# Filling TensorE's gaps in the opening of a Fourier-mixing and SoLU kernel with unread products, and moving two groups of real products

## The chip, the cores and the metric

The kernel runs on one core of one Trainium2 chip. The metric is the device time of one execution in microseconds (us). Before the change three runs gave 1123.95, 1124.88 and 1125.96 us, a median of 1124.88. The profile comes from one further execution.

Names of engines: PE is TensorE's matmuls, PEld its weight loads, DVE is VectorE, ACT is ScalarE, POOL is GpSimd, SP is the engine that only issues DMAs. A line such as L217 is a line of the kernel file.

## The reference

```python
X = np.fft.fft(x, axis=1)            # x: 8 x 3136 x 256
X = np.fft.fft(X, axis=2)
x = X.real.reshape(8 * 3136, 256)
h = x @ w_in                         # 256 x 1024
e = np.exp(h - max(h)); sm = e / (sum(e) + 1e-9)
solu = h * sm
ln = (solu - mean(solu)) / np.sqrt(var(solu) + 1e-6) * g_ln
out = ln @ w_out                     # 1024 x 256
```

Maximum, sum, mean and variance are taken over each row of 1024. The weights arrive in 64-bit floats, and the kernel itself turns them into 32-bit floats.

## The kernel before

The transform over the 3136 positions is split as 49 x 64. The eight batches are worked on in four pairs. The first pair's first transform is the opening of the kernel. It runs in eight **chunks** `c` = 0 to 7, one per turn of the loop `for c in range(NC)` (L823). In each turn DVE adds the mirrored half (`add_mirror`, L145 and L147) and folds the features into a tile `y` (`fold`: L152, L153, L165). PE then makes two products per chunk (`transform1`, L217; in the last chunk there is a small third tile `y0`). ACT copies each result out of PSUM (L220) into a tile `z`, and SP writes `z` to a DRAM tile `zd` (`keep`, L225). There are two `y` tiles in turn, so chunk `c` can only be folded once PE has read chunk `c - 2`. A product of 32-bit floats shows in the trace as two matmul instructions, called passes here: a chunk is 8 passes of some 256 columns.

DVE and ACT also convert the weights in the same loop: DVE takes `w_in` apart and puts it together (`exponent_in`, `narrow_in`, L586 to L636), with three ACT steps between (`confine`, L610 to L614). `w_out` follows after chunk 7 (`exponent_out`, `narrow_out`), in four pieces, into `Wo`. Piece 0 and 1 fill `Wo[:, 0:4]`, which is what the first half of the mean row reads.

The second matrix `Wi` is the Fourier matrix `Q` over the features times `w_in`. PE makes it with `product_in` (L690): `h` = 0 and `h` = 1 are four products of 512 columns each, numbered 0 to 3 by `parts`, and so is the middle row (`h` = KD = 2). Products `h` = 0 and the middle row use PSUM tile `h0`, `h` = 1 uses `h1`. ACT copies them out (`keep_in`, L694). The middle row's left operand lies in `w_mid`, written by ACT in `mid` (L681).

After the loop, `turn` (L233) reads `zd` back with the axes exchanged into a tile `g`: four DMAs on SP for the first two of five columns, four on POOL for the other three. `transform2` (L245) multiplies `g` by a table, ACT copies the result to `q` (L251), and `up` (L281) multiplies `q` by `Wi`: 4 passes of 512 columns into `h0`, 4 into `h1`. This is the start of a **unit**; there are 100 of them, as a rule with two tiles of 128 tokens each. On DVE a unit goes through `even` (L294), `join` (L302), `product` (L317), with ACT's `expo` (L310) and `square` (L324).

The program is under a manual schedule: each engine runs its instructions in the order in which the code issues them, and only semaphores between engines hold it up. So on PE everything behind a waiting matmul waits too.

`mean_out(0)` (L737) is four products of a matrix of ones by `Wo[:, 0:4]` into PSUM bank 3. It is the first half of the sum that `centre` later subtracts. `mean_out(1)` adds the second half after the first unit. In the kernel before, `mean_out(0)` stands after `begin(0)`, that is, behind unit 0's two `up`s and the `transform2` of unit 2, and ahead of `begin(1)`, which holds unit 1's `up`.

Of the kernel before, what the change touches and what calls it, by code (L numbers as in the profile page):

```python
# [9 lines left out]
FP32 = mybir.dt.float32  # L10
# [7 lines left out]
P = 128  # L18
# [26 lines left out]
def kernel(  # L45
# [19 lines left out]
    nc = tc.nc  # L65
    B, S, D = x.shape
    FF = moe_w_in.shape[1]
# [16 lines left out]
    ps_h = ctx.enter_context(tc.tile_pool(name="ps_h", bufs=1, space=PSUM))  # L84
# [11 lines left out]
    ident = const.tile([P, P], FP32, name="ident")  # L96
# [9 lines left out]
    def result(i):  # L106

        return banks[i % 4]
# [9 lines left out]
    def load(pr, c, room=None):  # L118

        r = slice(pr.p * PR, (pr.p + 1) * PR)  # L120
        rows = PR if pr.p else P
        if room is None:
            xa = xpool.tile([P, CH, D], FP32, tag="xa", name="xa")
            xb = xpool.tile([P, CH, D], FP32, tag="xb", name="xb")
        else:
            xa, xb = (t.rearrange("p (l d) -> p l d", d=D) for t in room)
        nc.sync.dma_start(out=xa[0:rows], in_=x_pn[r.start : r.start + rows, c * CH + 1 : (c + 1) * CH + 1, :])
        i = pr.p * NC + c
        nc.gpsimd.indirect_dma_start(
            out=xb[0:rows].rearrange("p l d -> p (l d)"), out_offset=None, in_=x_g,  # L130
            in_offset=bass.IndirectOffsetOnAxis(ap=idx[0:rows, i : i + 1], axis=0))
        xa, xb = xa[0:PR], xb[0:PR]
        x0 = None
        if c == NC - 1:
            x0 = xpool.tile([PR, 1, D], FP32, tag="x0", name="x0", bufs=1)
            nc.sync.dma_start(out=x0, in_=x_pn[r, 0:1, :])
        pr.raw[c] = (xa, xb, x0)

    def add_mirror(pr, c, engine, part=None):

        xa, xb, _ = pr.raw[c]
        rows = (0, CH) if part is None else (part * CH // 2, (part + 1) * CH // 2)
        r = slice(rows[0], min(rows[1], CH - 1 if c == NC - 1 else CH))
        a, rb = xa[:, r, :], xb[:, ::-1, :][:, r, :]
        i = engine.tensor_tensor(out=a[:, :, 1:D], in0=a[:, :, 1:D], in1=rb[:, :, D - 1 : 0 : -1], op=ALU.add)  # L145
        if part is None:
            engine.tensor_tensor(out=a[:, :, 0:1], in0=a[:, :, 0:1], in1=rb[:, :, 0:1], op=ALU.add)  # L147
        return i
# [6 lines left out]
    def fold(pr, c):  # L155

        xa, _, x0 = pr.raw.pop(c)
        pr.y[c] = xpool.tile([PR, CH, D], FP32, tag="y", name="y")
        sides = [(pr.y[c], xa)]
        if c == NC - 1:  # L160
            pr.y0 = xpool.tile([PR, 1, D], FP32, tag="y0", name="y0", bufs=1)
            sides.append((pr.y0, x0))
        for o, i in sides:
            fold_features(o, i)
            nc.vector.tensor_copy(out=o[:, :, 0:129:128], in_=i[:, :, 0:129:128])  # L165
# [21 lines left out]
    def transform1(pr, s):  # L187

        c, l = divmod(2 * s, CH)
        if s == 0:
            pr.zd = dram.tile([ZR, NH, D], FP32, tag="zd", name="zd")
        if l == 0:

            if pr.p or c < 2:
                pr.z = zpool.tile([ZR, CH, D], FP32, tag="z", name="z")
            elif c < 6:
                if c == 2:
                    pr.z_v = fpool.tile([P, 2, FF, 2], FP32, tag="v", name="z_v", bufs=2)  # L200
                pr.z = pr.z_v[0:ZR].rearrange("p a f b -> p (a f b)").rearrange("p (c l d) -> p c l d", c=4, l=CH)[:, c - 2]
            elif c == 6:
                pr.z = S_tiles[1][0:ZR, 0:2].rearrange("p a c k -> p (a c k)").rearrange("p (l d) -> p l d", l=CH)
            else:
                pr.z = gpool.tile([P, KG, D], FP32, tag="g", name="z_g")[0:ZR, 0:CH, :]
            pr.zs[c] = pr.z
        y = pr.y[c]
        ps = result(0 if pr.p else s).rearrange("p (l d) -> p l d", l=2)
        if s == NH // 2 - 1:
            parts = [(ps[0:ZR, 0], y[:, l], 0), (ps[0:ZR, 1], pr.y0[:, 0], 1), (ps[0:ZR, 1], y[:, l + 1], 2)]  # L210
        else:
            parts = [(ps[0:ZR], y[:, l : l + 2], 0)]
        pr.done.append(s)
        first = True
        for o, i, t in parts:
            for h, cs in enumerate((EVEN, ODD)):
                nc.tensor.matmul(o[..., cs], F[:, 2 * t + h, :], i[..., cs], start=first, stop=True,  # L217
                                 skip_group_check=True)
                first = False
        nc.scalar.copy(pr.z[:, l : l + 2, :], ps[0:ZR])  # L220
        if l == CH - 2:
            keep(pr, c, slice(0, ZR if pr.p else 4 * KG))
# [12 lines left out]
    def transform2(pr, k1, bank=0):  # L235

        i, k = divmod(k1, KG)
        g = pr.g[i]  # L240
        table = T[0][:, :, k, :] if i == 0 else T[1][:, :, k1 - KG, :]
        ps = result(bank)[:, 0 : KD * P]
        for h in range(KD):
            o = ps[:, h * P : (h + 1) * P].rearrange("p (b k) -> p b k", b=2)
            nc.tensor.matmul(o, g[:, k, h * P : (h + 1) * P], table,  # L245
                             start=(h == 0), stop=True, skip_group_check=True)
        return ps
# [324 lines left out]
    NW = 512  # L572
# [25 lines left out]
    def confine(unit, here=False, parts=(0, 1, 2)):  # L598

        if unit is None:  # L600
            return
        if here:
            bits(unit, unit, -896.0, ALU.add, 0.0, ALU.max)
            bits(unit, unit, 255.0, ALU.min, 2.0 ** 23, ALU.mult)
            return

        u = unit.bitcast(FP32)
        for i in parts:
            if i == 0:
                nc.scalar.activation(out=u, in_=unit, func=ACT.Relu, bias=limits[:, 0:1])  # L610
            elif i == 1:
                nc.scalar.activation(out=u, in_=u, func=ACT.Relu, bias=limits[:, 1:2], scale=-1.0)
            else:
                nc.scalar.activation(out=unit, in_=u, func=ACT.Identity, bias=limits[:, 2:3], scale=-(2.0 ** 23))  # L614
# [24 lines left out]
    class Weights:  # L639
# [43 lines left out]
        def product_in(self, h, parts=range(4), ps=None):  # L683
# [6 lines left out]
                nc.tensor.matmul(ps[:, fs], lhsT, self.w_in[c][:, fs], start=(c == 0), stop=(c == KD - 1))  # L690
            return ps

        def keep_in(self, h, ps):
            nc.scalar.copy(w_mid if h == KD else Wi[:, h, :], ps)  # L694

# [95 lines left out]
    with tc.manual_schedule():  # L791
        pairs = [Pair(p) for p in range(NP)]
        first, weights = pairs[0], Weights()
# [29 lines left out]
        for c in range(NC):  # L823

            if c == 0:
                weights.narrow_in(0)
                weights.narrow_in(1)
            elif c == 1:
                weights.narrow_in(2)
            add_mirror(first, c, nc.vector)  # L830
            if c == 0:
                weights.exponent_in(2)
            fold(first, c)
            if c == 1:
                weights.exponent_in(3)
            elif c == 2:
                weights.narrow_in(3)
            if c == NC - 1:
                for i in range(2):
                    weights.exponent_out(i)  # L840
                confine(weights.units[0], True)
                weights.narrow_out(0)
            if c + 6 < NC:
                load(first, c + 6)
            if c == 3:
                weights.place_out()
                for i in range(2):
                    weights.load_out(i)
                weights.load_table(0)
                weights.scale_out()  # L850
            for s in range(CH // 2):
                if c == NC - 1:
                    confine(weights.units[0], parts=(s,))
                transform1(first, c * CH // 2 + s)
            if c == 3:
                weights.mid()
            elif c == 5:
                weights.keep_in(0, weights.product_in(0))
            elif c == 6:
                odd = weights.product_in(1, (0, 1))  # L860

        turn(first, 0, nc.sync, 0, 2)
        turn(first, 0, nc.gpsimd, 2, KG)
# [10 lines left out]
        units = [Unit(p, k1) for p in range(NP) for k1 in range(NK)]  # L874
        for i in (1, 2):
            weights.narrow_out(i)
        pairs_q = [(t, transform2(pairs[0], t.k1, t.k1)) for t in units[:2]]
        confine(weights.units[0], parts=(0, 1))
        for (t, ps), part in zip(pairs_q, ((2,), ())):
# [29 lines left out]
        def begin(i):  # L909

            cur = units[i]
            enter(i)
            ps = up(cur, 0)
            if i in (2, 3):
                column(cur)
            even(cur, ps)
            cur.odd = up(cur, 1)
            second_transform(i + 2)
# [5 lines left out]

        batches = []
        begin(0)
        weights.mean_out(0)
        for i in range(whole + 1):
            cur = units[i]
            prv = units[i - 1] if i else None  # L930
# [242 lines left out]
```

## Time and profile before

| What | us |
|---|---|
| median of three runs | 1124.88 |
| the profiled execution | 1123.85 |
| its span, first to last instruction | 1122.1 |
| PE busy over the span | 1094.5 |
| DVE busy | 977.8 |
| ACT busy | 798.6 |
| POOL busy | 803.5 |
| PE's first matmul begins | 15.17 |
| unit 0's first `up` begins | 53.23 |

Busy time says how long an engine had an instruction in it, not how fast that instruction ran. [...]the time from one start to the next is the better measure of a stream. The first 60 us of the span are where all the edits lie.

### The profile page before, as it was taken

How to read it: one execution, taken by the hardware profiler on the slowest of the kernel's cores; microseconds unless marked ns; L12 is line 12 of the kernel's file. 1: busy time of each engine (PE TensorE's matmuls, PEld its weight loads, DVE VectorE, ACT ScalarE, POOL GpSimd, SP SyncE). 2: the span in 40 equal slices, each digit the busy share in tenths (PEclk: the TensorE clock that was granted, in tenths of full speed). 3: DMA queues.
4: the chain of work that ended last, by engine and by line, in shares of the span. 5: the costliest groups of instructions: out<-in, count | busy, mean ns of one | idle time of the engine just before them, and what ended most of it. 6: DMA issues, size and time to landing. Idle time of an engine off the chain costs nothing. (4 is left out here: it accounts for less than half of the span.)

```text
span 1122.1 us, 22005 instructions
## 1 busy us (share of the span) xinstructions
PE 1094.5 (98%) x7031; PEld 874.5 (78%) x7031; DVE 977.8 (87%) x1438; ACT 798.6 (71%) x1946; POOL 803.5 (72%) x709
## 2 busy tenths in 40 slices
PE   4999999999999999999999999999999999999998
PEld 2556878788777788787887787887877788778888
DVE  7889888989889889898889989898988899898884
ACT  4578777777766877777767777777776777777771
POOL 4057888767777879875876788876775676766664
PEclk9999999999999999999999999999999999999999
DMA  9574897766988979766898788876686875965655
GB/s 354 175 196 100 176 194 191 179 148 149 175 173 167 197 177 198 186 148 141 156 179 178 170 180 186 204 180 142 147 159 145 140 163 120 161 138 117 142 131 127
DMA packets 457930, 187.75 MB, mean 167 GB/s; under 512 B 424646, under 2 KB 439254, under 8 KB 457816
## 3 DMA queue, kind: packets, MB, share of 16 engines
q1 hardware_dynamic: 443800, 146.94, 62.2%
q0 software_dynamic: 14016, 39.40, 13.2%
q8 instruction: 57, 0.93, 0.3%
q14 instruction: 57, 0.47, 0.1%
HBM read 46.75 MB, written 38.80 MB: 76 GB/s over the span
## 5 line engine op out<-in xcount | busy, mean ns | idle before, releaser
L281 PE MATMUL ps_h<-Wi,q 128*128 128x512 f32 x800 | 361.6, 593 | 0.8 <-ACT q L251 0.4
L457 POOL TENSOR_TENSOR S<-uT 128x512 f32<-128x512 f32 x186 | 237.4, 1276 | 110.2 <-DVE u L317 30.7
L464 PE MATMUL ps_m<-Ws,S 128*128 128x128 f32 x2304 | 296.0, 275 | 0.0
L464 PEld LDWEIGHTS ps_m<-Ws,S 128*128 128x128 f32 x2304 | 279.5, 192 | 3.2 <-issue 0.2
L324 ACT ACTIVATE h<-u,usum 128x1024 f32<-128x1024 f32 x196 | 225.0, 1149 | 71.6 <-DVE u L317 71.6
L281 PEld LDWEIGHTS ps_h<-Wi,q 128*128 128x128 f32 x800 | 144.3, 190 | 145.4 <-issue 142.2
L317 DVE SCALAR_TENSOR_TENSOR u<-h,u 128x1024 f32<-128x1024 f32 x196 | 233.0, 1224 | 10.5 <-ACT u L310 10.5
L310 ACT ACTIVATE u<-h,nmax 128x1024 f32<-128x1024 f32 x196 | 223.2, 1140 | 2.3 <-DVE nmax L302 1.1
L388 DVE STREAM_TRANSPOSE v<-u 128x2048 f32<-128x2048 f32 x88 | 203.4, 2311 | 3.0
L464 PE MATMUL ps_m<-Wo,uT 128*128 128x128 f32 x1536 | 203.7, 276 | 0.3 <-DMA out_dram<-ot 0.3
L464 PEld LDWEIGHTS ps_m<-Wo,uT 128*128 128x128 f32 x1536 | 187.9, 192 | 1.4 <-issue 1.4
L302 DVE CUSTOM_DVE_ANT_0 h<-ev,ps_h 128x1024 f32<-128x1024 f32 x100 | 122.1, 1221 | 17.4 <-DVE ev L294 9.1
L302 DVE CUSTOM_DVE_ANT_0 h<-h,ps_h 128x1024 f32<-128x1024 f32 x96 | 117.2, 1221 | 14.2 <-ACT ot L508 0.5
L551 POOL DMA_INDIRECT out_dram<-ot,idx x96 | 107.3, 1118 | 28.4 <-issue 11.1
L294 DVE SCALAR_TENSOR_TENSOR ev<-w_mid,r,ps_h 128x1024 f32<-128x1024 f32 x99 | 122.8, 1240 | 2.7 <-PE ps_h L281 2.6
L457 POOL TENSOR_TENSOR S<-uT,S 128x512 f32<-128x512 f32 x93 | 118.8, 1277 | 7.2
L457 POOL TENSOR_TENSOR S<-S,uT 128x512 f32<-128x512 f32 x93 | 118.6, 1276 | 7.3
L464 PE MATMUL ps_m<-Ws,uT 128*128 128x128 f32 x768 | 101.8, 276 | 0.0
L464 PE MATMUL ps_m<-Wo,S 128*128 128x128 f32 x768 | 101.4, 275 | 0.0
L245 PEld LDWEIGHTS ps_m<-T,g 128*128 128x128 f32 x400 | 60.0, 191 | 49.3 <-issue 47.9
L499 ACT ACTIVATE ot<-ps_m,rs 128x256 f32<-128x256 f32 x96 | 45.5, 474 | 70.3 <-PE ps_m L464 50.3
L145 POOL TENSOR_TENSOR xa<-xa,xb 98x510 f32<-98x510 f32 (+1 forms) x48 | 59.5, 1240 | 48.0 <-DVE u L317 43.7
(111 smaller groups left out, 1244.0 us busy)
## 6 DMA issues: line engine op xcount, KB each, us to landing
uT<-v SPq DMA_DIRECT2D x752, 128.0 KB
g<-zd POOLq DMA_DIRECT2D x72, 160.0 KB, 5.3
out_dram<-ot SPq DMA_DIRECT2D x176, 64.0 KB
zd<-z SPq DMA_DIRECT2D x24, 400.0 KB
xa<-in_x_dram SPq DMA_DIRECT2D x24, 392.0 KB
raw_in<-in_moe_w_in_dram SPq DMA_DIRECT2D x4, 512.0 KB
xa<-in_x_dram SPq DMA_DIRECT2D x4, 512.0 KB
room<-in_x_dram SPq DMA_DIRECT2D x4, 512.0 KB
```

The source lines that it names most:

```text
L145: i = engine.tensor_tensor(out=a[:, :, 1:D], in0=a[:, :, 1:D], in1=rb[:, :, D - 1 : 0 : -1], op=ALU.add)
L245: nc.tensor.matmul(o, g[:, k, h * P : (h + 1) * P], table, start=(h == 0), stop=True, skip_group_check=True)
L281: nc.tensor.matmul(ps[:, fs], t.q[:, c * P : (c + 1) * P], Wi[:, c, fs], start=True, stop=not whole_even)
L294: nc.vector.scalar_tensor_tensor(out=t.ev, in0=w_mid, scalar=t.r, in1=ps, op0=ALU.mult, op1=ALU.add)
L302: nc.vector.tensor_tensor_reduce(out=t.h[s], in0=t.h[0] if s else t.ev, in1=t.odd, scale=1.0 if s else -0.5, scalar=3.0e38, op0=ALU.add, o ...
L310: nc.scalar.activation(out=t.u[s], in_=t.h[s], func=ACT.Exp, bias=t.nmax[:, s : s + 1], scale=-1.0, accum_out=t.esum[:, s : s + 1])
L317: t.last = nc.vector.scalar_tensor_tensor(out=t.u[s], in0=t.h[s], scalar=-1.0, in1=t.u[s], op0=ALU.mult, op1=ALU.mult, accum_out=t.usum[:, ...
L324: nc.scalar.activation(out=t.h[s], in_=t.u[s], func=ACT.Square, bias=t.usum[:, s : s + 1], scale=-float(FF), accum_out=t.ssq[:, s : s + 1])
L388: nc.vector.transpose(out=t.batch.v[:, :, t.w], in_=t.both.rearrange("p s (g n) -> p (s g) n", n=32))
L457: i = engine.tensor_tensor(out=S[j], in0=a, in1=b, op=op)
L464: nc.tensor.matmul(o, a[:, c], b[:, c], start=start and c == 0, stop=c == n - 1, skip_group_check=True)
L551: dma = nc.gpsimd.indirect_dma_start(out=out, out_offset=bass.IndirectOffsetOnAxis(ap=idx[:, i : i + 1], axis=0), in_=t.ot[s], in_offset=None)
```

## The change

```diff
+        def busy(self, n):
+            ps = ps_h.tile([P, FF], FP32, tag="h0", name="busy")
+            for _ in range(n):
+                nc.tensor.matmul(ps[:, 0 : NW // 2], ident, self.w_in[0][:, 0 : NW // 2], start=True, stop=True)
+
...
                 weights.load_table(0)
                 weights.scale_out()
+            if c < 4:
+                weights.busy((8, 4, 2, 5)[c])
             for s in range(CH // 2):
                 if c == NC - 1:
                     confine(weights.units[0], parts=(s,))
                 transform1(first, c * CH // 2 + s)
             if c == 3:
                 weights.mid()
+                weights.keep_in(0, weights.product_in(0))
+            elif c == 4:
+                odd = weights.product_in(1, (0,))
             elif c == 5:
-                weights.keep_in(0, weights.product_in(0))
-            elif c == 6:
-                odd = weights.product_in(1, (0, 1))
+                weights.product_in(1, (1,), odd)
...
         for i in (1, 2):
             weights.narrow_out(i)
+        weights.mean_out(0)
         pairs_q = [(t, transform2(pairs[0], t.k1, t.k1)) for t in units[:2]]
...
         begin(0)
-        weights.mean_out(0)
         for i in range(whole + 1):
```

There are three edits.

1. **Unread products.** Ahead of the real products of chunks 0, 1, 2 and 3, PE makes 8, 4, 2 and 5 products of the identity by the first 256 columns of `w_in[0]`. They go into PSUM tile `h0`, and nothing reads them.
2. **`w_in`'s products earlier.** `product_in(0)` and its copy move from behind chunk 5 to behind chunk 3. Parts 0 and 1 of `product_in(1)` move from behind chunk 6: part 0 to behind chunk 4, part 1 to behind chunk 5. Parts 2 and 3 and the middle row stay behind the loop.
3. **Mean row earlier.** `mean_out(0)` moves from behind `begin(0)` to ahead of the first two `transform2`s on PE.

## The prediction

> **What bounds the kernel now.** I read the page first, then PE's timeline of the first 60 us, then the same stretch on all engines, and last the table by stage and the waits beyond the opening.
>
> ```profile
> PE 1094.5 (98%) x7031; PEld 874.5 (78%) x7031; DVE 977.8 (87%) x1438; ACT 798.6 (71%) x1946; POOL 803.5 (72%) x709
> ...
> PEclk9999999999999999999999999999999999999999
> ```
> ```profile
> 100.00:1080.00 980.00, 978.36 (x6421) 790.20 (x6420) 871.31 (x1248) 718.53 (x1786) 735.79 (x635) 1.00 0.78 165
> ```
>
> From 100 to 1080 us PE is busy 978.36 of 980 us. There every engine follows PE, so what the opening saves should reach the end unchanged. The clock row says full speed everywhere. The timeline does not:
>
> ```profile
> 15.17 3.73 PE L217 MATMUL ps_m<-y,F 98*100 98x258 f32 x8 [15.17 <-DVE y L165]
> 20.33 7.34 PE L217 MATMUL ps_m<-y,F 98*100 98x258 f32 x16 [1.43 <-DVE y L165]
> 27.60 0.27 PE L710 MATMUL ps_m<-ident,gain 8*128 8x8 f32 x1
> 29.01 7.26 PE L217 MATMUL ps_m<-y,F 98*100 98x258 f32 x24 [1.14 <-DVE y L165]
> 36.11 3.60 PE L690 MATMUL wps<-w_in,Q 128*128 128x512 f32 x8
> 39.55 1.89 PE L217 MATMUL ps_m<-y,F 98*100 98x258 f32 x8
> 41.27 1.88 PE L690 MATMUL wps<-w_in,Q 128*128 128x512 f32 x4
> 42.99 2.34 PE L217 MATMUL ps_m<-y,F 98*100 98x258 f32 x16
> 45.18 1.88 PE L690 MATMUL wps<-w_in,Q 128*128 128x512 f32 x4
> 46.89 3.60 PE L690 MATMUL wps<-w_in,w_mid 128*128 128x512 f32 x8
> 51.65 1.13 PE L245 MATMUL ps_m<-T,g 128*128 128x128 f32 x8 [1.16 <-ACT w_mid L694]
> 53.23 3.70 PE L281 MATMUL ps_h<-Wi,q 128*128 128x512 f32 x8 [0.44 <-ACT q L251]
> 56.77 0.61 PE L245 MATMUL ps_m<-T,g 128*128 128x128 f32 x4
> 57.21 1.89 PE L737 MATMUL ps_m<-Wo,ones 128*128 128x256 f32 x8
> ```
>
> Eight passes take 3.73 us in chunk 0 and 1.89 us in chunk 6. From start to start a pass costs 0.427 us up to 32.5 us and 0.215 us from 32.9 us: PE runs at half speed until then. From 29.01 to 50.4 us it has no gap, so PE, slow for its first 3.6 us, is the bound there. Behind it, on the other engines:
>
> ```profile
> 45.37 0.59 ACT L220 COPY z_g<-ps_m 100x512 f32<-100x512 f32 x1
> ...
> 47.91 1.73 SPq L233 DMA_DIRECT2D g<-zd  x4
> ...
> 50.53 1.01 ACT L694 COPY w_mid<-wps 128x1024 f32<-128x1024 f32 x1 [0.29 <-PE wps L690]
> ...
> 52.82 0.35 ACT L251 COPY q<-ps_m 128x256 f32<-128x256 f32 x1
> ...
> 60.86 1.28 DVE L294 SCALAR_TENSOR_TENSOR ev<-w_mid,r,ps_h 128x1024 f32<-128x1024 f32 x1 [1.87 <-PE ps_h L281]
> ```
>
> The first transform2 (51.65) doesn't use w_mid. What it needs is g, whose four SP transfers the records show landing at 49.67, 50.23, 50.95 and 51.46. ACT, filled by the w_mid copy and two conversion steps, holds the q copy until 52.82. Unit 1's up starts only at 58.94, behind the mean row (57.21), and its even (60.86) finds DVE idle for 1.87 us. From there DVE has no idle longer than 0.2 us until 98 us (4.72 to 4.88 of each 5 us from 65 to 95, 4.65 in one), and then PE takes over.
>
> [...]20.33 to 27.5 us, with one gap of 0.09 us at 23.9, did not switch. [...]the last keep is issued at 45.99, and the turn that waits for it 1.92 us later.
>
> **The unread products.** They need the first piece of w_in, written by 9.40 us. Eight are 16 passes of 256 columns: 16 x 0.427 = 6.83 us slow, so from 9.45 to 16.3 at the latest, without a gap. [...]the switch falls between about 13 and 16.3. Chunk 0's y is ready at 15.11; its products are late by at most 1.2 us and take 8 x 0.215 = 1.72 instead of 3.42, so nothing behind is later. At the fast rate, 4, 2 and 5 products cost 1.71, 0.85 and 2.13 us. Chunk 1: y at 20.28, ends 22.05. Two products to 22.9. Chunk 2: y at 23.82, ends 25.6. Gain transpose and five products to 28.0. Chunk 3's y is ready at 28.87 as before, since DVE sets it. So the unread products lie wholly in waits, with idle gaps of 1.7, 0.9 and 0.9 us left. Does PE stay fast over 1.7 us? Before shows it for 1.2 us (50.4 to 51.65). If it falls back there, chunk 1 takes 3.42, and the queue behind pushes chunk 3 to about 30.2: 1.2 us lost. If not, nothing. I take nothing.
>
> **w_in's products.** The same passes in another order. From 29.01, all fast: chunks 3 to 6 are 4 x 1.72, chunk 7 is 2.19 (42.99 to 45.18), product_in(0) 3.44 (36.11 to 39.55), the two parts 1.72: sum 14.23. Before it was 45.18 - 29.01 = 16.17. So chunk 7 ends at 43.24, **1.94 us earlier**, if no y is late. Order: chunk 3 to 30.73, product_in(0) to 34.17, chunk 4 to 35.89, part 0 to 36.75, chunk 5 to 38.47, part 1 to 39.33, chunk 6 to 41.05. The price is on DVE, since y tiles come in two: chunk 6's fold waits for chunk 4 until 36.05 (before 35.35), chunk 7's for chunk 5 until 38.63 (before 37.68). DVE is 0.95 us later, but y is ready at 37.5 and 40.0 (y0 at 40.5), before PE wants it. Q has landed at 28.8 by the records, so mid and product_in(0) don't wait. keep_in(0) stands in ACT ahead of chunk 4's copies, 34.4 to 35.4; four banks cover that.
>
> Then each thing by its old distance: the last z copy 2.38 after chunk 7's start, at 43.4; g usable 6.28 after that (45.37 to 51.65), at 49.7; the w_mid copy, 3.64 after the middle row's start at 44.96, at 48.6, two ACT steps, q copy possible at 50.9. The late DVE has narrow_out(1) done at 48.1 (48.28 before; its 1.12 us wait for ACT takes up the delay).
>
> **The mean row.** Eight passes, 57.21 to 58.94 = 1.73 us. PE ends the middle row at 48.4 and Wo[:, 0:4] is ready at 48.1, so it runs 48.4 to 50.15. The wait for g, to 49.7, covers 1.3 of it and ACT the rest: transform2 from 50.15 gives q's source at about 50.8. Up begins at 51.3: **1.93 us earlier** than 53.23. If tracking were by whole tiles, it would wait for narrow_out(2) too, to 50.8, and 1.2 us would be lost; transform2 starting before POOL's part of g landed (52.7) speaks for parts. Removed from its old place, it lets unit 1's up follow transform2 at once: 51.3 + 3.54 + 0.44 = 55.28 against 58.94, and even(1) at +1.92 = 57.2. DVE gets there: join(0) 55.0 to 56.3, two narrow steps of 0.44 to 57.1. So even(1) is **3.66 us earlier** than 60.86.
>
> **Sum.** 1.94 + 1.72 = 3.66. Everything behind is DVE-bound, then PE-bound. The next suppliers have slack: fold_out on POOL moves with DVE; the second turn's g lands at 71.9 for a transform2 at 82.1; the next pair's loads land by 75.5 for a mirror at 83.8. SP's queue (keeps, table, turn) starts 1.9 earlier. Profiled execution: 1123.85 - 3.66 = 1120.2, span 1118.4. The median of the runs is 1.03 above that execution, so I forecast 1121.2.
>
> **Rivals.**
> Half the gain, either way (chance 0.19). If the clock falls back, chunks 3 to 7 take 16.17 again and only the mean row's 1.7 stays; if the mean row delays transform2 as much as it frees later, only 1.9 stays. For: the strictness seen at 23.9, and DVE being within 0.1 us of binding at even(1). Against: 16 gapless passes. Time 1123.0.
> Slower: the unread products run at half speed throughout (0.08). Place: PE ahead of chunk 3. From 9.45: 6.83, chunk 0 3.42, 3.42, chunk 1 3.42, 1.71, chunk 2 3.42, 0.2, 4.27: chunk 3 at 36.1 instead of 29.0. That is 7.1 later, less 1.7 for the mean row: 5.4 slower, 1130.3. It decides as soon as the queue ends after 28.87. For: the clock didn't rise in the 7.1 us from 20.33. Against: there was a gap in them.
> Absorbed (0.05): the opening ends early, but a transfer or POOL, 4.06 to 4.69 of 5 us busy around 90 to 100, sets the pace. Time 1124.5.
>
> **How the numbers follow.** The forecast case has 0.68, with 1119.2 (unit 1 gaining more, since DVE idled some 6 us between 40 and 60.86, and 1 us of run spread) to 1122.7 (the fallback's 1.2 us). Range 1119.0 to 1123.8: it takes in the half gain. Two tenths of a per cent are 2.25 us, about what a measurement tells from no change. Faster: 0.68 and the upper edge of the half gain; same: the rest of half and absorbed; slower: 0.08 and a little for the unseen.
>
> **What would show it.** L217 passes of 0.38 us, not 0.63, from chunk 0 or 1 on; chunk 3 starting at 29.0, chunk 7 ending near 43.2; DVE L152 waiting for PE near 36 and 38.6; L737 between the middle row and L245; up at 51.3; unit 1's L294 at 57.2. Wrong would be chunk 3 after 29.5, slow passes after 17 us, L245 later than 50.8, or an even gain at 100 us that is gone at 1100.

## The result, and the profile after

The changed kernel's median is 1120.21 us over six runs (1119.7 to 1120.9), beside 1124.84 us for six runs of the kernel before. The ratio is 0.9957, with a 95% interval from 0.9945 to 0.9969, so it is faster by 0.3 to 0.55%. The profiled execution took 1120.14 us, with a span of 1118.4 against 1122.1.

The page of the changed kernel, busy time per engine and the clock by slices, can't be told from that of before:

```profile
PE 1097.8 (98%) x7069; PEld 879.4 (79%) x7069; DVE 978.6 (87%) x1438; ACT 797.9 (71%) x1946; POOL 807.8 (72%) x709
...
PEclk9999999999999999999999999999999999999999
```

PE is even 3.3 us busier. From 100 to 1080 us its busy time is the same to the hundredth, so nothing points to a gain there (start and end, length, busy time of PE, PEld, DVE, ACT and POOL, clock, DMA share, GB/s):

```profile
100.00:1080.00 980.00, 978.36 (x6424) 790.46 (x6423) 871.93 (x1247) 716.47 (x1783) 739.09 (x636) 1.00 0.77 164
```

PE's timeline of the changed kernel (start, time, line, operation, passes, and in brackets the idle time before and its cause):

```profile
9.46 5.86 PE L696 MATMUL busy<-w_in,ident 128*128 128x256 f32 x16 [9.46 <-DVE w_in L636]
15.16 1.89 PE L217 MATMUL ps_m<-y,F 98*100 98x258 f32 x8
16.89 1.89 PE L696 MATMUL busy<-w_in,ident 128*128 128x256 f32 x8
20.25 1.97 PE L217 MATMUL ps_m<-y,F 98*100 98x258 f32 x8 [1.47 <-DVE y L165]
...
29.19 1.94 PE L217 MATMUL ps_m<-y,F 98*100 98x258 f32 x8 [0.59 <-DVE y L165]
30.97 3.60 PE L690 MATMUL wps<-w_in,Q 128*128 128x512 f32 x8
34.41 1.89 PE L217 MATMUL ps_m<-y,F 98*100 98x258 f32 x8
36.13 1.02 PE L690 MATMUL wps<-w_in,Q 128*128 128x512 f32 x2
37.00 1.89 PE L217 MATMUL ps_m<-y,F 98*100 98x258 f32 x8
38.72 1.02 PE L690 MATMUL wps<-w_in,Q 128*128 128x512 f32 x2
39.59 4.07 PE L217 MATMUL ps_m<-y,F 98*100 98x258 f32 x24
43.49 1.88 PE L690 MATMUL wps<-w_in,Q 128*128 128x512 f32 x4
45.21 3.60 PE L690 MATMUL wps<-w_in,w_mid 128*128 128x512 f32 x8
48.65 1.89 PE L742 MATMUL ps_m<-Wo,ones 128*128 128x256 f32 x8
50.37 1.05 PE L245 MATMUL ps_m<-T,g 128*128 128x128 f32 x8
51.54 3.70 PE L281 MATMUL ps_h<-Wi,q 128*128 128x512 f32 x8
```

Every chunk now takes 1.9 us. The passes speed up at 13.86, within the first sixteen: from start to start one costs 0.427 us ahead of that and 0.216 us behind it. Chunk 3 still starts when its y is ready (29.19, before 29.01), and chunk 7, the last sixteen passes of the x24 row, ends at 43.49 instead of 45.18. The first up comes at 51.54 instead of 53.23. On DVE the wait ahead of unit 1's even is gone (no bracket; before it was 1.87 us), and it starts at 57.45 instead of 60.86:

```profile
57.45 1.28 DVE L294 SCALAR_TENSOR_TENSOR ev<-w_mid,r,ps_h 128x1024 f32<-128x1024 f32 x1
```

DVE pays for the new order with two waits for PE, which holds the y tiles. The waits view of DVE from 30 to 62 us (what waited, for what, us in total, times, the longest):

```profile
DVE y L152 <- PE ps_m L217: 1.2, 2, 0.9
```

They cost the end nothing: PE has no wait ahead of chunks 4 to 7.

### The profile page after: what moved, and what is told of

It reads as the page before. It is cut to its first block, busy times and chain, and to the rows that moved or that the text cites. A ratio compares the mean times of both kernels' runs of the same rounds, so it can differ in the third digit from the quotient of the medians.

```text
span 1118.4 us, 22083 instructions
## 1 busy us (share of the span) xinstructions
PE 1097.8 (98%) x7069; PEld 879.4 (79%) x7069; DVE 978.6 (87%) x1438; ACT 797.9 (71%) x1946; POOL 807.8 (72%) x709
## 5 line engine op out<-in xcount | busy, mean ns | idle before, releaser
L464 PEld LDWEIGHTS ps_m<-Ws,uT 128*128 128x128 f32 x768 | 93.9, 192 | 0.0
```

The costliest lines, as they stand in the source:

```text
L464: nc.tensor.matmul(o, a[:, c], b[:, c], start=start and c == 0, stop=c == n - 1, skip_group_check=True)
```

## The experiments

Eleven kernels were run. Each profile falls into four stretches: the start of chunk 3, from there to the first up, from there to unit 1's even, and the rest of the span. The first stretch varies between the profiles: in e4 and e9 the first chunk started at 18.61 and 18.49, beside 15.16 in the changed kernel, with the same eight unread products ahead of it. So the profiles are compared by stretches, and the medians by their ratios to the kernel before.

| Kernel | Edits | chunk 3 starts | to first up | to even(1) | rest | ratio of the runs, 95% interval |
|---|---|---|---|---|---|---|
| before | | 29.01 | 24.22 | 7.63 | 1061.2 | 1 |
| after | products, order, mean | 29.19 | 22.35 | 5.91 | 1061.0 | 0.9957, 0.9945 to 0.9969 |
| e1 | products | 29.07 | 24.08 | 7.63 | 1061.0 | 0.9992, 0.9983 to 1.0002 |
| e2 | order | 28.83 | 25.62 | 7.63 | 1060.9 | 0.9992, 0.9985 to 0.9999 |
| e3 | mean | 29.03 | 24.24 | 5.90 | 1060.9 | 0.9979, 0.9969 to 0.9990 |
| e4 | products, order | 31.66 | 22.35 | 7.63 | 1061.1 | 0.9983, 0.9975 to 0.9990 |
| e5 | order, mean | 29.20 | 24.79 | 5.91 | 1061.7 | 0.9979, 0.9972 to 0.9985 |
| e6 | products, mean | 28.95 | 24.09 | 5.90 | 1061.6 | 0.9972, 0.9962 to 0.9982 |
| e7 | after, 8 products only | 29.00 | 24.05 | 5.90 | 1061.0 | 0.9983, 0.9974 to 0.9992 |
| e8 | after, without these 8 | 29.84 | 22.36 | 5.90 | 1062.6 | 0.9961, 0.9948 to 0.9974 |
| e9 | a real product in the wait | 32.05 | 19.72 | 5.91 | 1061.1 | 0.9937, 0.9924 to 0.9949 |
| e10 | e9, more filler | 30.66 | 19.33 | 5.91 | 1061.2 | 0.9948, 0.9934 to 0.9962 |
| e11 | after, filler past the wait | 30.19 | 22.30 | 5.90 | 1061.0 | 0.9970, 0.9960 to 0.9979 |

The spans add up from the four columns.

### One edit at a time, and the first two together

e1 has the calls of `busy` alone, e2 the moved `product_in` lines alone, e3 the moved `mean_out(0)` alone, e4 the first two. Against the changed kernel, e1 undoes these lines (e2 undoes the lower part, e3 the upper, and both drop the calls of `busy`; e4 undoes the lower part only):

```diff
             if c == 3:
                 weights.mid()
-                weights.keep_in(0, weights.product_in(0))
-            elif c == 4:
-                odd = weights.product_in(1, (0,))
             elif c == 5:
-                weights.product_in(1, (1,), odd)
+                weights.keep_in(0, weights.product_in(0))
+            elif c == 6:
+                odd = weights.product_in(1, (0, 1))
...
-        weights.mean_out(0)
         pairs_q = [(t, transform2(pairs[0], t.k1, t.k1)) for t in units[:2]]
...
         begin(0)
+        weights.mean_out(0)
```

> Only the unread products (8, 4, 2, 5) are added; w_in's products and the mean row stay where they were before. Theory 'joint': with fast passes PE catches up with DVE at once, chunks 4 and 5 wait for their y (31.6 and 34.2 us), chunk 5 ends near 35.9, almost as before (36.1), and product_in(0) behind it can't use the waits. Chunk 7 ends near 45.0, unit 0's up starts near 53.1, time about 1124.6 (gain 0.2). Rival 'separate', which is how the prediction's sum put it: the fast clock alone takes 1.9 us off PE's chain, chunk 7 ends near 43.3, up at 51.4, time about 1122.9.

> Only w_in's products are moved (behind chunks 3, 4, 5); no unread products, mean row as before. Both 'joint' and 'separate': PE is at half speed until about 32.7 us, has no gap from 29.0 on, and the sum of its passes is the same: chunk 7 ends at 45.2, up at 53.2, time about 1124.8 (0 to 0.4 slower, since DVE's folds of chunks 6 and 7 wait for PE and are some 2.8 us later). Rival 'the order does it': the waits filled by the order are worth 1.9 alone, 1122.9.

> Only the mean row is moved ahead of the first transform2. 'Joint' and 'separate' alike: PE ends the middle row at 50.4, the mean row 52.1, transform2 from 52.1 (0.5 later than before), but ACT holds the q copy to 52.8 anyway, so up starts at 53.3; unit 1's even comes at about 59.2 instead of 60.86. Time about 1123.2 (gain 1.65). Rival 'delays as much as it frees': even at 60.5, 1124.5.

> Unread products and moved w_in products; the mean row as before. 'Joint': chunk 7 ends near 43.5, up at 51.5, unit 1's even at 59.2, time about 1123.1 (gain 1.7), although e1 and e2 alone give about nothing. 'Separate': the same time, but then e1 must show it too.

Medians: e1 1124.14, e2 1125.1, e3 1123.07, e4 1123.81, beside 1125.51 of the kernel before in these runs. e1's PE timeline decides between the two theories:

```profile
29.07 1.94 PE L217 MATMUL ps_m<-y,F 98*100 98x258 f32 x8 [0.60 <-DVE y L165]
31.57 1.97 PE L217 MATMUL ps_m<-y,F 98*100 98x258 f32 x8 [0.56 <-DVE y L165]
34.26 1.94 PE L217 MATMUL ps_m<-y,F 98*100 98x258 f32 x8 [0.72 <-ACT z_v L220]
36.03 3.60 PE L690 MATMUL wps<-w_in,Q 128*128 128x512 f32 x8
```

PE is at full speed from chunk 0 on, and it only idles more: chunks 4 and 5 wait for their y, and product_in(0), which could run in these waits, stands behind them. (For chunk 5 the bracket names ACT's copy, which ended at 34.17; its y was complete at 34.11.) It starts at 36.03, before at 36.11. The faster PE, following DVE, gained 0.14 us up to the first up (24.08 for 24.22); that is 'joint', and 'separate' falls. e2 gains nothing in its profile, and loses 1.4 us there: PE was fast early in that execution but slow again in chunk 3 and most of product_in(0):

```profile
28.83 3.71 PE L217 MATMUL ps_m<-y,F 98*100 98x258 f32 x8 [2.10 <-DVE y L165]
32.33 5.14 PE L690 MATMUL wps<-w_in,Q 128*128 128x512 f32 x8
```

Its runs' ratio, 0.9992, hardly differs from 1. With both edits the stretch is 22.35 us (e4), 1.87 shorter than before. e3 takes 1.73 us off the stretch behind the up, and leaves the one ahead of it as it was (24.24): PE got to transform2 0.44 us later, at 52.09, but ACT held the q copy anyway, to 52.87 beside 52.82 before:

```profile
52.87 0.35 ACT L251 COPY q<-ps_m 128x256 f32<-128x256 f32 x1
```

'Delays as much as it frees' falls.

The runs alone would not have shown the coupling of the first two: e1, e2 and e4 stand at 0.9992, 0.9992 and 0.9983, with intervals wide enough for a plain sum. With the mean row in, they lean to it: e6 and e5, with one of the two, stand at 0.9972 and 0.9979, the changed kernel at 0.9957, 0.9979 without either (e3). That the first two edits need each other rests on the stretches of the profiles, one execution of each kernel.

### One edit taken out of the change

e5 is the changed kernel without `busy`, e6 with the old places of `product_in`.

> The changed kernel without the unread products. If the clock is what they bring: passes at 0.43 us until about 32.7 us, chunk 7 ends near 45.2, up at 53.2 to 53.5, unit 1's even at 59.2 to 59.5, time about 1123.2 (3 slower than the changed kernel's 1120.2). If they bring nothing: 1120.2.

> The changed kernel with w_in's products in their old places (behind chunks 5 and 6). 'Joint': chunk 7 ends near 45.0 because chunk 5 waits for its y and product_in(0) stands behind it; gain only that of the mean row and 0.2: about 1123.0. 'Separate': the order is worth nothing, 1120.3.

e5's median is 1122.94, e6's 1122.23, beside 1124.89. In e5 passes were slow until product_in(0) was under way, and the stretch is 24.79:

```profile
29.20 3.71 PE L217 MATMUL ps_m<-y,F 98*100 98x258 f32 x8 [1.14 <-DVE y L165]
32.70 4.32 PE L690 MATMUL wps<-w_in,Q 128*128 128x512 f32 x8
```

e6 has 24.09, as e1. Both profiles came out as 'joint' has it; e6's runs lie between its 1123.0 and the 1120.3 of 'separate'. Three of e5's 22 runs took 1120.17 to 1120.52, as little as the changed kernel, and the slowest 1124.97. No profile shows what was different in the three.

### Which unread products are needed

```diff
-                weights.busy((8, 4, 2, 5)[c])
+                weights.busy((8, 0, 0, 0)[c])      # e7
+                weights.busy((0, 4, 2, 5)[c])      # e8
+                weights.busy((8, 4, 2, 10)[c])     # e11
```

> The changed kernel with unread products (8, 0, 0, 0): the clock rises near 13.6 us as before, then PE idles about 3.3 us before chunk 1, 2.2 before chunk 2 and 3.0 before chunk 3. [...]passes stay at 0.215 and the time is that of the changed kernel, 1120.2; then the 4, 2 and 5 products are not needed. If gaps of 2 to 3 us are enough to fall back: chunk 1 or 2 shows 0.43 again, chunk 3 is slow, time about 1123.0.

> The changed kernel with unread products (0, 4, 2, 5). Chunk 0 is slow, 15.15 to 18.6, and the four products follow without a gap. If about 4 us without a gap raise the clock: it rises between 18.6 and 20, chunk 1 starts near 20.7 and is fast, chunk 3 starts at 29.2; time 1120.2, and the first eight are not needed. If the clock needs the longer run of 6.8 us or a full 128-row product: it rises later or not before chunk 3, time 1121 to 1123.

> The changed kernel with ten unread products ahead of chunk 3 in place of five: 2.13 us more at full speed, against some 0.8 us of wait left there. If unread products are free only inside the wait and chunk 3's start sets the end: chunk 3 starts near 30.5 instead of 29.2, up near 52.8, time about 1121.5 (1.3 slower than the changed kernel). If PE has slack behind chunk 3: no change, 1120.2.

e7's median is 1123.04, the higher of its two expected times (1120.2 and 1123.0): the gain of the first two edits is gone. Its PE timeline:

```profile
9.89 5.17 PE L696 MATMUL busy<-w_in,ident 128*128 128x256 f32 x16 [9.89 <-DVE w_in L636]
15.78 1.97 PE L217 MATMUL ps_m<-y,F 98*100 98x258 f32 x8 [0.71 <-DVE y L165]
20.83 6.51 PE L217 MATMUL ps_m<-y,F 98*100 98x258 f32 x16 [3.08 <-DVE y L165]
27.27 0.22 PE L715 MATMUL ps_m<-ident,gain 8*128 8x8 f32 x1
29.00 2.78 PE L217 MATMUL ps_m<-y,F 98*100 98x258 f32 x8 [1.52 <-DVE y L165]
31.58 4.49 PE L690 MATMUL wps<-w_in,Q 128*128 128x512 f32 x8
```

Chunk 0 is fast (1.97). After 3.08 us of idling chunks 1 and 2 take 6.51 together, nearly all of it slow. Chunk 3 begins fast and turns slow after 1.0 us (2.78), and product_in(0), 3.60 when fast, takes 4.49. So the products of chunks 1 to 3 together carry the gain: with them, in the changed kernel's profile, PE idled for at most 1.47 us at a time, and no pass turned slow again.

e8, without the first eight, has 1120.97 and a stretch of 22.36: chunk 0 is slow, the clock rises at 19.67 within the products behind it, and chunk 3 waits for its y as in the changed kernel. As far as five runs can tell (the intervals of e8 and the changed kernel nearly coincide), the first eight aren't needed.

```profile
15.70 3.74 PE L217 MATMUL ps_m<-y,F 98*100 98x258 f32 x8 [15.70 <-DVE y L165]
19.23 2.12 PE L696 MATMUL busy<-w_in,ident 128*128 128x256 f32 x8
```

e11's median is 1122.07. Chunk 3 starts at 30.19, 1.0 us later than in the changed kernel, and the span is 1.0 longer (1119.4). Expected were 1.3. Chunk 3 now follows the filler without a wait:

```profile
25.77 4.58 PE L696 MATMUL busy<-w_in,ident 128*128 128x256 f32 x20
30.19 1.89 PE L217 MATMUL ps_m<-y,F 98*100 98x258 f32 x8
```

Here the unread products were free only inside the wait, and the 1.0 us by which chunk 3 started later went straight to the end.

### A version that takes work out of the chain

e9 fills the wait ahead of chunk 3 with product_in(0) in place of the five unread products. For this, the load of Q (`load_tables`) is issued behind chunk 3's load instead of chunk 5's, and part 2 of product_in(1) moves behind chunk 6. These were not tried one by one. e10 adds filler ahead of chunks 1 and 2.

```diff
             load(first, c, rooms.get(c))
             if c == 2:
                 weights.piece_in(3)
-        weights.load_tables()
+            if c == 3:
+                weights.load_tables()
...
-            if c < 4:
-                weights.busy((8, 4, 2, 5)[c])
+            if c < 3:
+                weights.busy((8, 4, 2)[c])         # e10: (8, 8, 4)
+            elif c == 3:
+                weights.keep_in(0, weights.product_in(0))
...
-                weights.keep_in(0, weights.product_in(0))
             elif c == 4:
                 odd = weights.product_in(1, (0,))
             elif c == 5:
                 weights.product_in(1, (1,), odd)
+            elif c == 6:
+                weights.product_in(1, (2,), odd)
...
-        weights.product_in(1, (2, 3), odd)
+        weights.product_in(1, (3,), odd)
```

> The changed kernel, but the wait ahead of chunk 3 is filled by product_in(0) itself (3.44 us, real work) in place of the five unread products; for this the load of Q is issued behind chunk 3's load and not behind chunk 5's; and part 2 of product_in(1) goes behind chunk 6. Counts 8, 4, 2 for chunks 0 to 2 stay. Theory: what the changed kernel still pays is PE's gapless chain from chunk 3 to the first up, 22.35 us; taking 3.44 us of it into a wait of some 2.7 us lets chunk 3 start near 29.9 instead of 29.2 and gives some 2.5 us, of which DVE, which feeds chunk 7 only at 39.4 to 39.8, takes back about 1: chunk 7 ends near 41.9 instead of 43.5, up at 50.0 instead of 51.5, unit 1's even at 56.0, time about 1118.7. Rival 'DVE is now the bound' (its conversion of w_out can't come earlier): up no earlier than 51.2, time 1120.0. Rival 'the earlier Q delays the loads of chunks 4 and 5': chunk 4 or 5 starts late, 1120.5.

> As e9, with 8 and 4 unread products ahead of chunks 1 and 2 instead of 4 and 2, so that the gaps of 1.6 and 1.2 us there nearly close. If gaps under 1.7 us don't bring half speed back: same time as e9, 1118.7. If they sometimes do (in e7 a gap of 1.67 us was followed by slow passes): the median falls by up to 0.5 and the spread of the runs narrows. If the longer filler holds up chunk 1 or 2: chunk 1 starts up to 0.3 later, nothing behind it moves.

e9's median is 1118.72, as expected, beside 1125.9. Its profiled execution began late and is the slowest of its six runs (1120.58), but from chunk 3 to the first up it took 19.72 us, where about 20.1 were expected:

```profile
28.51 3.70 PE L690 MATMUL wps<-w_in,Q 128*128 128x512 f32 x8
32.05 3.96 PE L217 MATMUL ps_m<-y,F 98*100 98x258 f32 x16
```

e10's median is 1119.78 with about the same spread (1118.44 to 1121.06, e9 1118.04 to 1120.58), so the extra filler brought nothing that could be told. From e10's PE timeline:

```profile
27.15 3.67 PE L690 MATMUL wps<-w_in,Q 128*128 128x512 f32 x8 [0.34 <-DMA Q<-in_q_tab_dram]
30.66 3.62 PE L217 MATMUL ps_m<-y,F 98*100 98x258 f32 x16
...
46.67 1.89 PE L742 MATMUL ps_m<-Wo,ones 128*128 128x256 f32 x8
48.85 1.13 PE L245 MATMUL ps_m<-T,g 128*128 128x128 f32 x8 [0.29 <-DMA g<-zd]
49.99 2.41 PE L281 MATMUL ps_h<-Wi,q 128*128 128x512 f32 x5
```

Up comes at 49.99, 1.55 us earlier than in the changed kernel, though chunk 3 starts 1.47 later. The bound has changed: transform2 now waits for g, the turn through DRAM behind chunk 7. Of e9 and the changed kernel, which ran beside different runs of the kernel before, the intervals (0.9924 to 0.9949 and 0.9945 to 0.9969) just overlap.

## Why the prediction was right

The forecast was 1121.2 us, a gain of 3.66. The profiled execution gained 3.71, and the steps below are about that one. The medians of the runs are 4.63 apart, with an interval of some 3.5 to 6.2, and 1121.2 lies above all six runs of the changed kernel. The forecast had added 1.03 us, by which the median of before stood above its profiled execution; in the changed kernel that difference was 0.07. So the size fits the profiled execution closely, while the runs bear it out only within their noise. By its steps:

- **The unread products** lie in waits, as forecast. The clock rose at 13.86. The forecast, between about 13 and 16.3, was an estimate from the 3.6 us of gapless passes ahead of the rise before, counted from 9.45, and from the end of sixteen slow passes. Chunk 0 wasn't late, and chunk 3 came at 29.19 for 28.9 to 29.0. The 0.18 there need be no cost of the change: DVE waited 0.77 us for the last piece of w_in, before 0.51. The risk of 1.2 us, falling back in the gap ahead of chunk 1, didn't come true with its 1.47 us of idling in that execution. The forecast took it at nothing without showing why; e4 and e7, where passes were slow behind gaps of 1.93 and 3.08 us, show that it was real, and e7's chunk 3, which turned slow 0.96 us behind a gap of 1.52 us, how near it was.
- **The chain of chunks.** The sum was 14.23 us from chunk 3 to the end of chunk 7, measured 14.30. The DVE folds were to wait until 36.05 and 38.63; they waited until 36.34 and 38.93, 0.3 later, 0.18 of it because chunk 3 was late. So the part to the first up, 1.93 forecast, was 1.87 from chunk 3 on, and 1.69 on the clock of the span.
- **What the working left out.** It called the new order "the same passes in another order" and took 1.94 from the faster passes, "if no y is late". It didn't ask whether y would be late in the old order. e1 shows that it is, and that the fast clock alone gains 0.14 in that stretch. The sum holds only because both edits are there.
- **The mean row.** 1.73 forecast, 1.72 to 1.73 measured (7.63 to 5.91, and e3). Its place ahead of transform2 was to be covered by the wait for g and by ACT; e3's profile shows both. PE never waited for Wo.
- **Carried to the end.** even(1) was 3.41 earlier (3.66 forecast, the difference being chunk 3's 0.18 and 0.07 behind it). The rest took 1061.0 for 1061.2, within what the other profiles show (1060.9 to 1061.7, and 1062.6 in e8, which nothing here explains). That adds 0.29 and makes 3.70. 'Absorbed' falls.
- **Rivals.** 'Half the gain' didn't come true for the changed kernel, but its size was right: e5 without unread products and e7, where the clock fell back, have 1122.94 and 1123.04 where it said 1123.0. 'Unread products at half speed throughout' didn't happen in any profile.
- **A reason was not borne out.** "The strictness seen at 23.9" rested on one stretch of the chunks' passes, slow from 20.33 to 27.5 us with 0.09 us of idling in it. That the 0.09 us kept the clock down was not shown. Unread products brought a rise after as little as 2.81 (e6), 2.86 (e10) and 3.01 us (e7).

## What to carry to other kernels

Ask of a faster engine what it will wait for next: here full speed was worth nothing until work that needed no new data was put into the waits it opened. In e11 filler that nobody reads, free up to the next arrival, delayed chunk 3 and the end by 1.0 us once it reached beyond it; real work moved into the wait did better: e9's median is 1.5 us below the changed kernel's, though their intervals just overlap. Judge TensorE's speed by the time from the start of one pass to the next (of 258 columns 0.427 us slow, 0.215 us fast), not by its busy share (98% before and after).

## What was not expected of the hardware

- **The clock column hides a slow start.** It shows 1.00 for the kernel before, whose passes were at half speed until 32.8 us (0.427 us from start to start, then 0.215). Half speed shows in it only after a first rise, in e2, e4 (0.90 from 15 to 20 us, 0.76 from 20 to 25) and e7. In e7 (start and end of the window, its length, busy time of PE, PEld, DVE, ACT and POOL, clock, DMA share, GB/s) the first line's passes are slow, though it says 1.00:

```profile
9.48:12.90 3.42, 3.00 (x7) 2.50 (x8) 2.88 (x6) 0.78 (x2) 3.36 (x3) 1.00 1.02 396
12.90:16.31 3.41, 2.69 (x13) 1.97 (x13) 3.38 (x8) 1.90 (x3) 1.95 (x2) 1.00 1.03 411
16.31:19.72 3.41, 1.44 (x7) 0.82 (x5) 3.38 (x6) 1.43 (x3) 0.14 (x1) 1.00 1.02 408
19.72:23.14 3.42, 2.31 (x6) 1.63 (x7) 3.39 (x8) 1.83 (x3) 1.05 (x1) 0.50 1.04 413
23.14:26.55 3.41, 3.41 (x10) 2.32 (x9) 3.34 (x7) 1.64 (x4) 0.00 (x0) 0.50 1.02 406
26.55:29.96 3.41, 1.89 (x10) 1.23 (x9) 3.38 (x7) 1.00 (x3) 0.00 (x0) 1.00 1.05 400
29.96:33.38 3.42, 3.42 (x8) 1.90 (x7) 3.37 (x9) 1.76 (x4) 0.00 (x0) 0.50 1.02 385
```

- **In e2, e4 and e7 the clock's changes lay 3.41 us or twice that apart.** e7's changes, at 12.90, 19.72, 26.55, 29.96 and 33.38, lie 3.41 or 6.83 us apart, and so do those of e2 (25.19, 28.60, 35.43) and e4 (15.59, 19.00, 22.42), to within 0.01. Where they lie differs from profile to profile: with eight unread products at the start the first rise came between 12.68 (e10) and 16.06 us (e11), that is 2.86 and 6.00 us after the first of them began. In the 3.41 us ahead of the falls PE was busy for 1.44 and 1.89 (e7), 1.48 (e4) and 1.54 us (e2). The length of a gap alone decided nothing: passes stayed fast behind one of 2.60 us (e9) and were slow behind one of 1.93 (e4). What decides was not shown.

- **The same two chunks sped up in one profile and not in three.** Without unread products chunks 1 and 2 took 7.34 us before, 7.30 in e3 and 7.33 in e5, slow throughout, and 5.91 in e2, where the clock rose at 25.19. What set e2 apart was not shown. The chunks' passes are 98*100 in the timelines, the unread ones 128*128. Whether that matters wasn't tried.
